# A third buffer for pair maxima, identity products moved behind a dense piece, and squares parted from their relu, in a fused top-k attention and squared-relu kernel

## The chip, the cores and the metric

The kernel runs on one core of one Trainium2 chip. A core has TensorE (PE in the profile, with its weight loads as PEld), VectorE (DVE), ScalarE (ACT), GpSimd (POOL) and SyncE (SP), which here only starts transfers. The metric is the device time of one execution in microseconds (us), the median of several runs. Lower is better.

## What is computed

For each of 8 x 8 heads with 576 rows of 64, scores are formed, all but the 32 largest of a row are dropped, and a softmax weighs the values. The result, as 4608 rows of 512, goes through two dense layers with a squared relu between them. Cut to what matters:

```python
scores = scale * np.matmul(q, k.transpose(0, 1, 3, 2))
kth = np.partition(scores, -32, axis=-1)[..., -32:-31]
scores = np.where(scores >= kth, scores, -1e9)
attn = softmax(scores)
x = np.matmul(attn, v)          # as (4608, 512)
h = np.maximum(x @ w_in, 0.0)   # w_in 512 x 2048
out = (h * h) @ w_out           # w_out 2048 x 512
```

## The kernel before

The attention is cut into 144 steps. A step is two blocks of 128 query rows (two heads of a pair, for one chunk c of the rows; a leftover chunk of 64 rows takes two pairs at once), each with 576 scores per row. The list `steps` (line 168) goes through the batches; U is 144, Z is 125, DEEP is 9. The loop of line 662 runs steps 0 to 124, the loop of line 750 the steps of the last batch, and what follows is written out by hand. Every instruction is pinned, so each engine executes its instructions in the order in which the Python code issues them. There is no scheduler to reorder them. What is decided by a planner is small: the two counters `debt` estimate how busy GpSimd and ScalarE are, and choose whether some small jobs go to one or the other engine (lines 223, 242, 504).

The pieces of a step that matter here:

- `scores` (line 193): TensorE forms the right half of the scores in the PSUM bank pair `sc_b` and the left half in `sc_a`. ScalarE copies both into the SBUF tile `s` (line 208), first the right half, `copy(1)`, then the left, `copy(0)`. In between, while the next step's right half has just been formed, TensorE also multiplies the upper half of `tops` of the step before with an identity (lines 202 to 204), which puts it into a spare region of `sc_b` called `far` (line 97).
- `split` (line 221): VectorE takes the elementwise maximum of the left half, still in `sc_a`, and the right half, in `s`, into the tile `tops` (line 231). In 131 steps this is one instruction for all 288 pairs (the step is marked `lent`, and its upper half is brought to `far` by the identity products); in 13 it is three smaller ones, which write `far` directly (lines 233 to 236).
- `join` (line 240): VectorE takes maxima, and in some steps minima, of `far` and the lower half of `tops` into `cat` (line 246). So `cat` begins with maxima of four scores each.
- `joint_mins` and `small_mins` (lines 248, 255): GpSimd computes the minima that belong to these maxima, as integer sum minus maximum. It reads `tops` (lines 252, 260), and line 253 reads the first quarter of `cat`.
- `topk` (line 268): VectorE finds the 32 largest in four rounds of eight, with a MAX8 (line 278) and a replace (line 282) for each head, over windows of `cat` that grow from 104 to 576 elements.
- `below` and `expo` (lines 322, 330): ScalarE computes the marks of dropped scores and the exponentials; GpSimd adds both (`mask`, line 326), SyncE transposes them by a transfer (`turn`), TensorE multiplies with the values (`products`, line 645), VectorE inverts the sums (line 396), and ScalarE puts the result into `x_tok` (line 421).
- The dense layers run as pieces between these: `up` (line 488, TensorE at line 495), then on ScalarE a relu into `rl` (line 501), then a square into `h2`, 82 times on ScalarE (line 506) and otherwise on GpSimd (line 509); `down` (line 517) multiplies with `w_out`, and ScalarE copies the result out. `dense` (line 558) issues one or two pieces, or an idle piece that only keeps TensorE running (line 542). A relu that is due waits in the list `late` until the next `flush` (line 346).

In the steps from 12 to 124, the order of issue is: first `below` of the step before, `split(u+2)`, `scores(u+3)`, `topk` round 0, placing of finished rows, GpSimd's minima, a dense piece, second `below`, `topk` rounds 1 to 3, `join(u+2)`, exponentials and mask of the step before, another dense piece, value products of step u-3. In the loop of line 750 the scores come after the mask, then the value products, one piece, the last rounds of `topk`, `join`, and two or three pieces.

`tops` has two buffers, so `split(u)` has to wait until the readers of `tops` of step u-2 are done. `s` has five buffers, `cat` three, `x_tok` eight.

Of the kernel before, what the change touches and what calls it, by code (L numbers as in the profile page):

```python
# [22 lines left out]
def kernel(  # L23
# [169 lines left out]
    def scores(u):  # L193
        for j in (1, 0):
            rest = steps[u][0][1] == 4
            for x, g in ((0, 0), (1, 1), (0, 1), (1, 0)) if rest else ((0, steps[u][0][2]), (1, steps[u][1][2])):
                i, c, _ = steps[u][x]
                qkT = prep[i][0]
                r = slice(64 * g, 64 * g + 64)
                pin(nc.tensor.matmul(out=sc[j][r if rest else slice(0, 128), x, 0:HALF], lhsT=qkT[r, 0, c * 128:min(S, (c + 1) * 128)],  # L200
                                     rhs=qkT[r, 1, j * HALF:(j + 1) * HALF], start=True, stop=True))
            if j and u > 1 and "lent" in st[u - 1]:
                for x in range(2):
                    pin(nc.tensor.matmul(out=far[:, x, :], lhsT=id_f[:, :], rhs=st[u - 1]["tops"][:, x, QUAR:HALF], start=True, stop=True))  # L204
        s = scp.tile([128, 2, S], f32, name="s", bufs=5)

        def copy(j):
            pin(nc.scalar.activation(s[:, :, j * HALF:(j + 1) * HALF], sc[j][:, :, 0:HALF], AF.Copy))  # L208
        st[u] = {"s": s}
        copy(1)  # L210
        if u < 2:
            st[u]["rest"] = lambda: copy(0)
        else:
            copy(0)
        for i, c, a in steps[u]:
            qk_left[i] -= 1

    def split(u):
        d = st[u]
        lend = (2 < u < U - 20 and debt["G"] < 4.9 and debt["A"] < 5.4) or Z < u < U - 5
        cat = d["cat"] = scp.tile([128, 2, S], f32, name="cat", bufs=3)
        tops = d["tops"] = scp.tile([128, 2, HALF], f32, name="tops", bufs=2)
        one, two = sc[0][:, :, 0:HALF], d["s"][:, :, HALF:S]
# [95 lines left out]
    def below(u, x):  # L322
        d = st[u]
        pin(nc.scalar.activation(marks[u % 2][:, x, :], d["s"][:, x, :], AF.Relu, bias=d["m"][3][:, x, 7:8], scale=-1.0))  # L324

    def mask(u):
# [3 lines left out]
    def expo(u, x):  # L330
        d = st[u]
        pin(nc.scalar.activation(w_two[u % 3][:, x, 0:S], d["s"][:, x, :], AF.Exp, bias=d["low"][:, x, :], scale=DROP))

    def exps(u):
# [3 lines left out]

    late, squares = [], []
    hold = {"squares": False, "out": False}  # L340
# [72 lines left out]
    def place(u):  # L413
        for x, (i, c, a) in enumerate(steps[u]):
            b, pr = pairs[i]
            o, r = st[u]["o"][:, x, :], st[u]["r"]
            if c < 4:
                if (b, c) not in x_tok:
                    x_tok[b, c] = ffp.tile([128, 512], bf16, name="x_tok", bufs=8)
                h = 2 * pr + a  # L420
# [62 lines left out]
    def block(xt, stores):  # L483
# [4 lines left out]
        def up(f0):  # L488
            def go():
# [9 lines left out]
                def bend():  # L499
# [4 lines left out]
                    if DEEP + 15 < now[0] < Z and debt["A"] < 5.4 and debt["G"] > 5.0:  # L504
                        owe(A=0.62)
                        late.append(lambda: pin(nc.scalar.activation(h2, flat, AF.Square)))
                        return
# [154 lines left out]
    for u in range(Z):  # L662
# [18 lines left out]
        if u == DEEP + 2:  # L681
            join(u + 1)
            split(u + 2)
            ahead(u + 3)
        if ok(f) and f % 2:
            invert_two(f)
# [8 lines left out]
        elif u != DEEP + 1:  # L695
            small_mins(u + lead)
        dense(u, 0)
        if u > 0:
            below(u - 1, 1)
# [4 lines left out]
            if u == DEEP + 1:  # L704
                split(u + 2)
                small_mins(u + 2)
                ahead(u + 3)
            topk(u, (3,))
            if u == DEEP:
# [19 lines left out]
        if u == DEEP:  # L729
            small_mins(u + 2)  # L730
            ahead(u + 3)
        for _ in range(2 if u < 8 or u in (U - 22, U - 19) else 1):
            prepare(u)
# [16 lines left out]
    for u in range(Z, U - 2):  # L750
# [25 lines left out]
        if not piece():  # L776
            idle_piece()
        topk(u, (2, 3))
        join(u + 2)
# [286 lines left out]
```

## Time and profile before

| | us |
|---|---|
| median of 3 runs | 893.45 (892.72 to 898.47) |
| profiled execution | 895.84 |
| its span, from first to last instruction | 893.9 |
| VectorE busy | 852.5 (95%) |
| ScalarE busy | 816.5 (91%) |
| TensorE busy | 789.3 (88%) |
| GpSimd busy | 789.4 (88%) |
| mean granted clock of TensorE | 0.979 |

Busy time is the time in which an engine executes something. A row of the view of groups gives line, engine, operation, tiles and shapes, then busy time and mean duration in ns, then the engine's idle time just before, and what ended it. A row of the view of waits says which engine and line waited for which, with the total in us, the number of times and the longest. A row of the timeline gives start and duration in us, engine, line, operation, tiles; in brackets the idle time of the engine before it and what ended that. A row of the view by stretches gives, for a part of the span, the busy time and number of instructions of each engine, the granted clock of TensorE (PEclk, 1.00 is full), and what the DMA engines did. Neighbouring instructions on ScalarE and VectorE overlap a little in these records.

### The profile page before, as it was taken

The numbers are of one execution on the slowest core, as the hardware profiler recorded it, in microseconds if no ns is written. First come the engines' busy times: TensorE is split into PE (matmuls) and PEld (weight loads), VectorE is DVE, ScalarE is ACT, GpSimd is POOL, SyncE is SP. The second block draws the span as 40 slices with busy tenths as digits, with TensorE's granted clock in tenths as the row PEclk, the third lists the DMA queues.
The fourth block names the chain that finished last, engine by engine and source line by source line (L and its number), as shares of the span: only waits on it lengthen the run. The fifth ranks groups of instructions, "written<-read, shape, count | busy, mean of one in ns | idle before, by whom it ended". The sixth has DMA issues, their size and how long they took to land.

```text
span 893.9 us, 19858 instructions
## 1 busy us (share of the span) xinstructions
PE 789.3 (88%) x5950; PEld 485.6 (54%) x6030; DVE 852.5 (95%) x3455; ACT 816.5 (91%) x1617; POOL 789.4 (88%) x745
## 2 busy tenths in 40 slices
PE   6999997889888888899889888898998998999975
PEld 3455555556555555555555555555555654656654
DVE  5999999999999999999999999999999989999994
ACT  3888999899999999999999999999999999888973
POOL 3778999999999999999999999999999878999861
PEclk8999999999999999999999999999999989999999
DMA  5597875754555556355555554455565554423431
GB/s 119 127 219 158 176 164 104 117 102 98 102 106 106 117 118 116 67 108 118 118 117 111 107 116 91 97 111 117 118 124 111 104 95 92 81 61 81 71 82 43
DMA packets 325443, 98.05 MB, mean 110 GB/s; under 512 B 317520, under 2 KB 317776, under 8 KB 325328
## 3 DMA queue, kind: packets, MB, share of 16 engines
q1 hardware_dynamic: 323984, 96.28, 53.3%
q8 instruction: 49, 0.80, 0.4%
q10 hardware_dynamic: 1344, 0.43, 0.2%
q14 instruction: 66, 0.54, 0.2%
HBM read 36.70 MB, written 9.44 MB: 52 GB/s over the span
## 4 chain that ended last, share of the span: by engine, by line
DVE 48%; PE 19%; POOL 10%; ACT 9%; issue 6%; DMA 2%; SPq 0%; POOLq 0%; ACTq 0%; DVEq 0%
DVE m L278 20%; DVE cat L282 16%; DVE tops L231 6%; DVE cat L246 4%; PE av_ps L393 3%; PE sc_b L200 3%; PE gen L495 3%; ACT s L208 2%; PE sc_b L204 2%; PE sc_a L200 2%; POOL cat L259 2%; PE dn_ps L545 2%; PE dn_ps L523 2%; POOL cat L260 2%; ACT marks_b L324 1%
## 5 line engine op out<-in xcount | busy, mean ns | idle before, releaser
L278 DVE MAX8 m<-cat 128x8 f32<-128x104 f32 (+3 forms) x1152 | 444.0, 433 | 0.0
L282 DVE MATCH_REPLACE8 cat<-m,cat 128x104 f32<-128x104 f32 (+2 forms) x864 | 265.7, 320 | 0.3 <-issue 0.3
L260 POOL TENSOR_TENSOR cat<-cat,tops 128x576 int32<-128x576 int32 (+1 forms) x144 | 195.0, 1354 | 13.0 <-DVE tops L234 1.8
L259 POOL TENSOR_TENSOR cat<-s 128x576 int32<-128x576 int32 (+1 forms) x144 | 195.0, 1354 | 6.5 <-ACT s L208 6.5
L393 PEld LDWEIGHTS <-wT 128*128 128x128 bf16 (+3 forms) x1600 | 97.5, 99 | 93.9 <-issue 51.1
L200 PE MATMUL sc_b<-qkT 64*128 64x288 f32 (+1 forms) x640 | 121.1, 454 | 29.4 <-DVE cat L246 20.9
L523 PE MATMUL dn_ps<-w_out,h 128*128 128x512 bf16 x494 | 132.4, 384 | 11.4 <-issue 5.6
L495 PEld LDWEIGHTS <-w_in 128*128 128x128 bf16 x1344 | 111.5, 98 | 45.0 <-issue 19.3
L495 PE MATMUL gen<-xT,w_in 128*128 128x256 bf16 (+1 forms) x1088 | 128.6, 266 | 1.3 <-ACT xT L455 0.7
L200 PE MATMUL sc_a<-qkT 64*128 64x288 f32 (+1 forms) x640 | 117.5, 453 | 0.0
L208 ACT ACTIVATE s<-sc_b 128x576 f32<-128x576 f32 x144 | 92.9, 645 | 26.6 <-PE sc_b L204 12.7
L324 ACT ACTIVATE marks_a<-s,m 128x576 bf16<-128x576 f32 x144 | 111.7, 784 | 0.0
L324 ACT ACTIVATE marks_b<-s,m 128x576 bf16<-128x576 f32 x142 | 109.6, 780 | 0.0
L231 DVE TENSOR_TENSOR tops<-sc_a,s 128x576 f32<-128x576 f32 x131 | 99.7, 761 | 5.3 <-POOL cat L252 4.0
L208 ACT ACTIVATE s<-sc_a 128x576 f32<-128x576 f32 x144 | 93.7, 651 | 11.1 <-PE sc_a L200 7.4
L204 PE MATMUL sc_b<-tops,id_f 128*128 128x144 f32 x524 | 101.7, 318 | 0.9 <-DVE tops L231 0.9
L204 PEld LDWEIGHTS sc_b<-tops,id_f 128*128 128x128 f32 x524 | 73.0, 193 | 54.0 <-DVE m L278 20.7
L246 DVE TENSOR_TENSOR cat<-sc_b,tops 128x288 f32<-128x288 f32 x217 | 92.1, 456 | 5.2 <-ACT s L208 5.1
L523 PEld LDWEIGHTS <-h 128*128 128x128 bf16 x560 | 48.1, 98 | 69.0 <-issue 31.2
L501 ACT ACTIVATE rl<-gen 128x512 f32<-128x512 f32 x140 | 83.3, 595 | 2.4 <-PE gen L495 2.4
L200 PEld LDWEIGHTS sc_b<-qkT 64*128 64x128 f32 (+1 forms) x640 | 49.1, 178 | 55.4 <-DVE cat L246 26.5
L282 DVE MATCH_VALUE_LOAD cat<-m,cat 128x8 f32 x864 | 75.8, 88 | 0.0
(137 smaller groups left out, 1319.4 us busy)
## 6 DMA issues: line engine op xcount, KB each, us to landing
out_dram<-wide SPq DMA_DIRECT2D x31, 256.0 KB, 2.6
q_raw<-in_q_dram SPq DMA_DIRECT2D x30, 256.0 KB, 3.6
k_raw<-in_k_dram SPq DMA_DIRECT2D x30, 256.0 KB, 3.7
v_raw<-in_v_dram SPq DMA_DIRECT2D x30, 256.0 KB, 4.1
h<-in_moe_w_in_dram SPq DMA_DIRECT2D x8, 512.0 KB, 5.3
h<-in_moe_w_out_dram SPq DMA_DIRECT2D x8, 512.0 KB, 4.3
out_dram<-wide SPq DMA_DIRECT2D x9, 128.0 KB, 2.4
q_raw<-in_q_dram SPq DMA_DIRECT2D x32, 32.0 KB, 3.1
```

The costliest lines, as they stand in the source:

```text
L200: pin(nc.tensor.matmul(out=sc[j][r if rest else slice(0, 128), x, 0:HALF], lhsT=qkT[r, 0, c * 128:min(S, (c + 1) * 128)], rhs=qkT[r, 1, j ...
L204: pin(nc.tensor.matmul(out=far[:, x, :], lhsT=id_f[:, :], rhs=st[u - 1]["tops"][:, x, QUAR:HALF], start=True, stop=True))
L208: pin(nc.scalar.activation(s[:, :, j * HALF:(j + 1) * HALF], sc[j][:, :, 0:HALF], AF.Copy))
L231: pin(tt(tops[:, :, :], one, two, op=ALU.max))
L246: pin(nc.vector.tensor_tensor(d["cat"][:, :, lo:lo + QUAR], far, d["tops"][:, :, 0:QUAR], op=op))
L259: pin(nc.gpsimd.tensor_tensor(at, s[:, :, 0:n].bitcast(i32), s[:, :, HALF:HALF + n].bitcast(i32), op=ALU.add))
L260: pin(nc.gpsimd.tensor_tensor(at, at, d["tops"][:, :, 0:n].bitcast(i32), op=ALU.subtract))
L278: pin(nc.vector.max(out=m[r][:, x, :], in_=cat[:, x, at]))
L282: pin(nc.vector.match_replace(out=cat[:, x, at], in_to_replace=m[r][:, x, :], in_values=cat[:, x, at], imm_value=NEG))
L324: pin(nc.scalar.activation(marks[u % 2][:, x, :], d["s"][:, x, :], AF.Relu, bias=d["m"][3][:, x, 7:8], scale=-1.0))
L495: pin(nc.tensor.matmul(out=hp[:, n * n_rows:(n + 1) * n_rows], lhsT=w_in[:, kh, (f0 + n) * 128:(f0 + n + 1) * 128], rhs=xt(kh), start=(kh ...
L523: pin(nc.tensor.matmul(out=op[:, :], lhsT=held["h2"][:, f, c * 128:(c + 1) * 128], rhs=w_out[:, f, :], start=(f == 0), stop=(f == NF - 1)))
```

## The change

Three edits. The tile `tops` gets a third buffer, and `x_tok` gives one up. The identity products leave `scores` for a function `bring`, which is called behind the first dense piece of a step (and at the matching places of the first steps and of the loop of line 750), so that they come after both halves of the scores and after that piece. A square that goes to ScalarE is no longer issued right behind its relu but by `follow`, which the next `below` or `expo` calls after its own instruction.

```diff
@@ scores
-            if j and u > 1 and "lent" in st[u - 1]:
-                for x in range(2):
-                    pin(nc.tensor.matmul(out=far[:, x, :], lhsT=id_f[:, :], rhs=st[u - 1]["tops"][:, x, QUAR:HALF], start=True, stop=True))
+    def bring(w):
+        if w > 0 and "lent" in st[w]:
+            for x in range(2):
+                pin(nc.tensor.matmul(out=far[:, x, :], lhsT=id_f[:, :], rhs=st[w]["tops"][:, x, QUAR:HALF], start=True, stop=True))
@@ split
-        tops = d["tops"] = scp.tile([128, 2, HALF], f32, name="tops", bufs=2)
+        tops = d["tops"] = scp.tile([128, 2, HALF], f32, name="tops", bufs=3)
@@ below and expo, at the end of each
+        follow()
@@
-    late, squares = [], []
+    late, later, squares = [], [], []
+
+    def follow():
+        while later:
+            later.pop(0)()
@@ place
-                    x_tok[b, c] = ffp.tile([128, 512], bf16, name="x_tok", bufs=8)
+                    x_tok[b, c] = ffp.tile([128, 512], bf16, name="x_tok", bufs=7)
@@ bend
-                        late.append(lambda: pin(nc.scalar.activation(h2, flat, AF.Square)))
+                        later.append(lambda: pin(nc.scalar.activation(h2, flat, AF.Square)))
@@ loop of steps 0 to Z-1
             ahead(u + 3)
+            bring(u + 2)
...
         dense(u, 0)
+        if u and not DEEP < u < DEEP + 3:
+            bring(u + lead)
...
                 ahead(u + 3)
+                bring(u + 2)
...
             ahead(u + 3)
+            bring(u + 2)
@@ loop of steps Z to U-3
         products(u - 2)
         if not piece():
             idle_piece()
+        bring(u + 2)
         topk(u, (2, 3))
         join(u + 2)
```

More of the change, by code (lines that the diff above doesn't have):

```diff
@@ L332, in expo @@
         pin(nc.scalar.activation(w_two[u % 3][:, x, 0:S], d["s"][:, x, :], AF.Exp, bias=d["low"][:, x, :], scale=DROP))
+        follow()
     def exps(u):
```

## The prediction

> **What bounds the kernel now.** The page comes first, then busy time by stretch. The span is cut at 24, 100, 757, 830 and 870 us: start, weight loading, the long middle, the last batch's loop from line 750, the tail.
>
> ```profile
> span 893.9 us, 19858 instructions
> ```
>
> ```profile
> core 0: us, PE busy (x) PEld busy (x) DVE busy (x) ACT busy (x) POOL busy (x), PEclk, DMA share, GB/s
> 24.00:100.00 76.00, 72.25 (x465) 37.98 (x470) 73.93 (x294) 64.63 (x120) 62.20 (x54) 1.00 0.80 177
> 100.00:757.00 657.00, 582.37 (x4371) 360.81 (x4429) 646.12 (x2633) 637.62 (x1265) 618.51 (x572) 0.98 0.55 110
> 757.00:830.00 73.00, 68.44 (x555) 43.93 (x562) 67.99 (x280) 62.28 (x128) 69.00 (x60) 0.98 0.33 69
> ```
>
> In the middle VectorE (DVE) works 646.1 of 657 us, ScalarE (ACT) 637.6, GpSimd (POOL) 618.5. VectorE sets the pace; ScalarE is 8.5 us behind it. VectorE's own work is unchanged: in the built programs its instructions, GpSimd's and SyncE's stand in the same order before and after. So the change can only act on VectorE's idle time, and the middle holds 657 - 646.1 = 10.9 us of that. The waits of VectorE in that stretch say whom it waits for:
>
> ```profile
> DVE tops L231 <- POOL cat L252: 4.0, 8, 1.4
> DVE shares L404 <- PE av_ps L393: 2.8, 4, 2.2
> DVE cat L246 <- ACT s L208: 1.7, 3, 0.9
> DVE tops L231 <- ACT s L208: 0.9, 3, 0.5
> ```
>
> 4.0 us is what the third buffer aims at, 1.7 + 0.9 = 2.6 us what a lighter ScalarE could give back, 2.8 us is TensorE's. A gain of 1% is 8.9 us, about what a measurement of this kernel can tell from no change; 4.0 + 2.6 = 6.6 does not reach it.
>
> **Third buffer for the pair maxima (line 225).** It removes the wait of split for the reader of the tile two steps back. The longest of the eight:
>
> ```profile
> 234.34 0.80 POOL L252 TENSOR_TENSOR cat<-tops 128x288 int32<-128x288 int32 x1
> ...
> 235.17 0.76 DVE L231 TENSOR_TENSOR tops<-sc_a,s 128x576 f32<-128x576 f32 x1 [1.35 <-POOL cat L252]
> ...
> 235.22 0.79 POOL L253 TENSOR_TENSOR cat<-cat 128x288 int32<-128x288 int32 x1
> ...
> 236.29 0.25 DVE L282 MATCH_REPLACE8 cat<-m,cat 128x104 f32<-128x104 f32 x1
> ```
>
> What is late next stands in the same rows: L253 reads the first quarter of cat, which L282 overwrites. L253 ends at 236.01; L282 started at 236.29. So the replace may move up by 0.28 us, not by 1.35, and the rest becomes a wait of L282 for L253. Eight times 0.28 is 2.2 us at most if GpSimd keeps its time; all 4.0 if it comes earlier; 0 if its lag sits elsewhere. GpSimd does come a little earlier, since it waits for ScalarE's exponentials and 33 of the 82 squares now stand behind the second of these instead of between the two. I take -2.5 us. The tile x_tok pays with one buffer of its eight. A batch fills four, so at seven a buffer returns seven fillings later, by when the tile before it has long been transposed: 0 (bounds 0 and, should SyncE's queue be late once, +0.5).
>
> **Squares apart from their relu (lines 339, 506).** All 82 squares leave the place right behind their relu:
>
> ```profile
> L506 ACT ACTIVATE h<-rl 128x512 bf16<-128x512 f32 x82 | 51.8, 632 | 2.6
> ```
>
> ```profile
> 403.81 0.57 ACT L501 ACTIVATE rl<-gen 128x512 f32<-128x512 f32 x1
> ...
> 404.42 0.63 ACT L506 ACTIVATE h<-rl 128x512 bf16<-128x512 f32 x1
> ...
> 404.96 0.58 ACT L135 ACTIVATE qkT<-gen 128x512 f32<-128x512 f32 x1
> ...
> 405.43 0.77 ACT L324 ACTIVATE marks_b<-s,m 128x576 bf16<-128x576 f32 x1
> ```
>
> Relu to square takes 404.42 - 403.81 = 0.61 us from start to start; the equally long copy L135 hands over in 405.43 - 404.96 = 0.47, since there nothing is needed from the instruction before. The square pays 0.14 us each time: 82 x 0.14 = 11.5 us off ScalarE's 637.6. On VectorE's path only the 2.6 us above can come back; bounds 0 and -2.6, and I take -1.5, because part of the 2.6 belongs to stretches where TensorE, not ScalarE, was late. In 49 of the 82 cases the square now stands between line 324 and the copy of sc_b. It was ahead of both before, so that copy is no later. A square comes out later by up to a microsecond; the down product that reads it stands pieces behind and, in the built program, no down product waits for a ScalarE square by itself: 0 (up to +0.5 if one piece came to wait).
>
> **Identity products behind the first dense piece (lines 202 to 204 into bring).** 131 pairs of matmuls move; no DMA does. Their work is the same, their neighbours change. The copy of sc_b no longer waits for them, so ScalarE gains some of this:
>
> ```profile
> ACT s L208 <- PE sc_b L204: 12.7, 18, 1.5
> ```
>
> But the join (L246) still needs them, and all three parts of a bank are kept apart: in the built program the moved product waits for ScalarE's copy of sc_b, and the join for the moved product as well as the copy. Before, the join followed the copy at once:
>
> ```profile
> 325.99 0.64 ACT L208 ACTIVATE s<-sc_b 128x576 f32<-128x576 f32 x1
> ...
> 326.66 0.46 DVE L246 TENSOR_TENSOR cat<-sc_b,tops 128x288 f32<-128x288 f32 x1 [0.49 <-ACT s L208]
> ```
>
> Copy end 326.63, join 326.66. Now the product, 0.76 us by the rows below, stands between them with a second hand-over: 0.03 + 0.76 + 0.03, so about 0.8 us more, up to 1.2 if the 0.39 us that TensorE loses ahead of such weights counts too. What is queued behind the waiting product on TensorE is the second dense piece, the value products and the next scores; these wait for ScalarE's x_tok copy anyway, which follows the same copy of sc_b, so I charge them nothing extra. Followed through the timeline, 41 of the 112 joins from 98 to 751 us start less than 0.9 us behind the end of the copy, the first and the last of them these:
>
> ```profile
> 113.98 0.64 ACT L208 ACTIVATE s<-sc_b 128x576 f32<-128x576 f32 x1
> ...
> 115.39 0.47 DVE L246 TENSOR_TENSOR cat<-sc_b,tops 128x288 f32<-128x288 f32 x1
> ...
> 736.97 0.65 ACT L208 ACTIVATE s<-sc_b 128x576 f32<-128x576 f32 x1
> ...
> 738.09 0.45 DVE L246 TENSOR_TENSOR cat<-sc_b,tops 128x288 f32<-128x288 f32 x1
> ```
>
> They are bunched in some seven bouts in which ScalarE falls behind. If ScalarE fell behind as before, each bout would cost up to 0.8 once: 7 x 0.8 = 5.6 us. It does not: 0.14 us a square over eight to ten squares a bout is 1.1 to 1.4 us more room than the 0.8 taken. I take +1.0 for the bouts where TensorE is late instead, bounds 0 and +5.6.
>
> By the Trainium skill, page PSUM — Partial Sum Buffer, section PSUM bank collisions raise a hardware error, any two engines must be kept apart on one bank, whatever columns they touch. By that rule nobody could drop the new wait while far lies in sc_b's bank; the trace agrees with a join that reads other columns than the copy and yet waits for it, and the sum stays the one made here from rows.
>
> Two places show a price that ScalarE's room doesn't pay. At the start, TensorE is the chain:
>
> ```profile
> 45.23 0.76 PE L200 MATMUL sc_b<-qkT 64*128 64x288 f32 x4 [0.87 <-ACT qkT L146]
> ...
> 45.91 0.76 PE L204 MATMUL sc_b<-tops,id_f 128*128 128x144 f32 x4
> ...
> 46.60 0.76 PE L200 MATMUL sc_a<-qkT 64*128 64x288 f32 x4
> ...
> 47.29 2.12 PE L545 MATMUL dn_ps<-fill,id_h 128*128 128x512 bf16 x7
> ...
> 47.44 0.82 DVE L246 TENSOR_TENSOR cat<-sc_b,tops 128x288 f32<-128x288 f32 x2
> ```
>
> L545 is two idle pieces of 1.06. In the new order sc_a ends at 46.67, the first idle piece at 47.7, the product at 48.4: the join comes 1.0 us later than 47.44. TensorE's pace is unchanged, so this shifts VectorE once: +0.9 (bounds 0 and +1.5).
>
> In the last batch's loop the product stands behind products and a piece:
>
> ```profile
> 826.73 0.76 PE L200 MATMUL sc_b<-qkT 64*128 64x288 f32 x4
> ...
> 827.41 0.76 PE L204 MATMUL sc_b<-tops,id_f 128*128 128x144 f32 x4
> ...
> 828.79 0.79 PE L393 MATMUL av_ps<-vau_a,wT 128*128 128x65 bf16 x10
> ...
> 828.89 0.82 DVE L246 TENSOR_TENSOR cat<-sc_b,tops 128x288 f32<-128x288 f32 x2 [1.02 <-ACT s L208]
> ...
> 829.74 0.81 PE L523 MATMUL dn_ps<-w_out,h 128*128 128x512 bf16 x3 [0.16 <-issue]
> ```
>
> Same work, product last: it ends where L523 ends now, 830.55, and the join starts at 830.6 instead of 828.89: 1.7 us later. TensorE works 68.4 of 73 us here and has two or three pieces to do before it needs that join, so the delay does not repeat. It is one shift, +1.6 us (bounds 0, if VectorE catches up in the tail, and +2.4), and nothing behind hides it.
>
> **Sum.** -2.5 - 1.5 + 1.0 + 0.9 + 1.6 = -0.5 us. The profiled execution took 895.84 us (1.9 around its span), so 895.3 for one like it; it lies 2.4 above the median of 893.45, and against the median I predict 893.0.
>
> **Rivals.** *Slower:* ScalarE's 11.5 us are eaten elsewhere (its lag comes from what it waits for) and the product behind the copy sets every tight join. It speaks for it that ScalarE waits for TensorE too:
>
> ```profile
> ACT s L208 <- PE sc_a L200: 7.4, 16, 0.6
> ```
>
> Price 5.6 for the bouts, 1.5 and 2.4 at the ends, gains halved (-2): 893.45 + 7.5 = 901; beyond 1% once the bouts cost over 7 us. *Faster:* GpSimd and ScalarE come early enough to clear all 6.6 us of the middle, and the ends cost 1.0: 888. For it stands ScalarE's room, against it L253 above. *The clock:* TensorE's granted clock falls to half after some poorly filled windows:
>
> ```profile
> 514.30:517.70 3.40, 1.64 (x16) 0.82 (x15) 3.40 (x11) 3.40 (x9) 3.32 (x4) 1.00 0.51 113
> 517.70:521.10 3.40, 3.40 (x22) 2.09 (x20) 3.40 (x19) 3.33 (x8) 3.32 (x4) 0.51 0.32 63
> 719.10:725.90 6.80, 6.80 (x26) 3.56 (x26) 6.28 (x26) 5.83 (x12) 6.46 (x8) 0.50 0.50 78
> ```
>
> A wait in the middle of a step splits TensorE's idle time, and windows could fill better or worse. The stretch at 719 cost VectorE 6.80 - 6.28 = 0.5 itself and at most the 2.2 us wait in the L404 row behind it. Two more such stretches give 893.0 + 5 = 898, two fewer 888. The Trainium skill, page TensorE: Matmul & The Clock Gate, section Part 1: The HAM clock gate (the "warmup" mystery), asks for an idle window of about 3.4 us; the trace differs, the window at 514.3 was busy 1.64 of 3.40 us. By the page's rule a step that never idles that long could not change the clock at all.
>
> **How the numbers follow.** Forecast 0.56 (its own range 889.5 to 896.5), slower rival 0.20, faster rival 0.16, clock 0.08. Half of the slower rival passes 902.4 (1% over), and a little of the clock: 0.11. A fifth of the faster one passes 884.5: 0.03. The remaining 0.86 is within 1%. The range takes the faster rival's 888 less a microsecond of its bounds and the slower one's 901: 887 to 901.
>
> **What would show it.** Right: the tops row for L252 gone, a new, shorter wait of L282 for L253; relu to next instruction 0.47; a join waiting for the product at line 221, in the first 60 us and from 757; VectorE busy 852.5 as before. Wrong: VectorE's idle time in the middle above 12 us with joins waiting for line 221 throughout (then the room argument fails), or under 5 us (then L253 was no limit).

## The result and the profile after

The changed kernel takes 885.01 us (median of 5 runs, 881.30 to 886.72), the kernel before in the same session 893.45 (5 runs, 891.56 to 899.90). The ratio is 0.9881, with a 95% interval of 0.9832 to 0.9931. Run again beside later experiments it took 882.41 us against 896.80, ratio 0.9841 (0.9802 to 0.9881). So it is 1.2 to 1.6% faster. Predicted were 893.0 us, a range of 887 to 901, and 0.03 for faster by over 1%: the prediction was wrong.

The profiled execution took 881.3 us, the fastest of its five; the profiled one of the kernel before, 895.84, lies above its median. So the two traces differ by more than the medians. From the page of the changed kernel:

```profile
span 879.4 us, 20006 instructions
...
PE 767.8 (87%) x6030; PEld 483.7 (55%) x6030; DVE 849.1 (97%) x3455; ACT 804.6 (91%) x1617; POOL 788.5 (90%) x745
```

ScalarE's 816.5 us of work became 804.6, and VectorE's 852.5 became 849.1. The view by stretches, cut as before:

```profile
24.00:100.00 76.00, 70.95 (x476) 40.14 (x476) 74.02 (x298) 64.42 (x122) 63.00 (x54) 0.98 0.81 178
100.00:757.00 657.00, 573.88 (x4510) 362.85 (x4507) 653.89 (x2678) 637.35 (x1286) 628.03 (x584) 0.99 0.57 112
757.00:830.00 73.00, 69.32 (x615) 47.74 (x614) 69.50 (x285) 63.55 (x130) 68.95 (x59) 0.98 0.35 71
```

In the middle VectorE is now idle for 657 - 653.89 = 3.1 us instead of 10.9, and in the same time it issues 2678 instructions instead of 2633. Most of the gain lies there. All that VectorE waits for in that stretch, by the view of waits:

```profile
DVE cat L248 <- PE sc_b L221: 2.2, 1, 2.2
```

The waits for GpSimd (4.0 us), for ScalarE (2.6) and for the value products (2.8) are gone; one wait for a moved product is new. ScalarE's own waits in that stretch:

```profile
ACT s L205 <- DVE cat L284: 7.7, 6, 2.6
ACT s L205 <- PE sc_a L200: 3.0, 9, 0.8
```

Before, no row of the first kind stood above 0.4 us in the middle. It does not mean what its name says. A wait for several engines is put down to the one that came last, and the place at 234 us shows the order:

```profile
231.97 0.80 DVE L248 TENSOR_TENSOR cat<-sc_b,tops 128x288 f32<-128x288 f32 x2
...
232.83 1.19 PE L200 MATMUL sc_b<-qkT 64*64 64x288 f32 x8 [1.37 <-DVE cat L248]
...
234.12 0.65 ACT L205 ACTIVATE s<-sc_b 128x576 f32<-128x576 f32 x1 [1.36 <-DVE cat L284]
```

TensorE may form the next right half only when VectorE's join has read `sc_b` (or, in a step that is not lent, when its split has written there): here it starts 0.06 us behind the join's end at 232.77. The copy starts 0.10 us behind the end of these scores at 234.02. In all 11 idle times above 0.15 us ahead of this copy in the middle the order is the same. So ScalarE has run ahead until only VectorE's hold on `sc_b` stops it. The five buffers of `s` are not the limit.

The place of the longest wait that the prediction quoted (1.35 us at 235.17) shows how far GpSimd has come forward. From the timeline of the changed kernel:

```profile
229.90 0.80 POOL L254 TENSOR_TENSOR cat<-tops 128x288 int32<-128x288 int32 x1
...
230.78 0.80 POOL L255 TENSOR_TENSOR cat<-cat 128x288 int32<-128x288 int32 x1
...
232.69 0.75 DVE L233 TENSOR_TENSOR tops<-sc_a,s 128x576 f32<-128x576 f32 x1
```

Before, the split stood idle until GpSimd's add ended at 235.14. Now the add ends 2.0 us and the subtract behind it 1.1 us before the split starts, and the replace that the prediction named as the next limit (line 284 here) starts at 233.80, 2.2 us behind the subtract. With the third buffer alone the add at this place ended at 234.41 and the split started at 234.40: GpSimd was still late.

### The profile page after: what moved, and what is told of

It reads as the page before. It is cut to its first block, busy times and chain, and to the rows that moved or that the text cites. A ratio compares the mean times of both kernels' runs of the same rounds, so it can differ in the third digit from the quotient of the medians.

```text
span 879.4 us, 20006 instructions
## 1 busy us (share of the span) xinstructions
PE 767.8 (87%) x6030; PEld 483.7 (55%) x6030; DVE 849.1 (97%) x3455; ACT 804.6 (91%) x1617; POOL 788.5 (90%) x745
## 4 chain that ended last, share of the span: by engine, by line
DVE 65%; PE 18%; issue 8%; ACT 4%; POOL 2%; DMA 2%; SPq 0%; DVEq 0%; ACTq 0%; POOLq 0%
DVE m L280 28%; DVE cat L284 19%; DVE cat L248 8%; DVE tops L233 7%; PE gen L504 4%; PE dn_ps L532 4%; PE sc_b L200 3%; PE sc_b L221 2%; PE sc_a L200 2%; PE av_ps L402 2%; ACT s L205 1%; DMA wT<-w_two_b 1%; DVE sc_b L235 1%; PE dn_ps L554 1%; POOL cat L261 1%
## 5 line engine op out<-in xcount | busy, mean ns | idle before, releaser
L280 DVE MAX8 m<-cat 128x8 f32<-128x104 f32 (+3 forms) x1152 | 437.2, 421 | 0.1
L284 DVE MATCH_REPLACE8 cat<-m,cat 128x104 f32<-128x104 f32 (+2 forms) x864 | 261.4, 310 | 0.1
L262 POOL TENSOR_TENSOR cat<-cat,tops 128x576 int32<-128x576 int32 (+1 forms) x144 | 194.9, 1353 | 15.5 <-DVE tops L236 2.9
L200 PE MATMUL sc_b<-qkT 64*128 64x288 f32 (+1 forms) x640 | 118.2, 452 | 64.1 <-DVE cat L248 49.1
L532 PE MATMUL dn_ps<-w_out,h 128*128 128x512 bf16 x560 | 145.2, 385 | 3.8 <-ACT wide L542 3.7
L326 ACT ACTIVATE marks_a<-s,m 128x576 bf16<-128x576 f32 x144 | 115.3, 809 | 0.0
L221 PE MATMUL sc_b<-tops,id_f 128*128 128x144 f32 x524 | 94.7, 304 | 22.4 <-ACT s L205 21.7
L200 PE MATMUL sc_a<-qkT 64*128 64x288 f32 (+1 forms) x640 | 112.4, 434 | 0.1
L221 PEld LDWEIGHTS sc_b<-tops,id_f 128*128 128x128 f32 x524 | 75.4, 193 | 57.5 <-ACT s L205 52.2
L233 DVE TENSOR_TENSOR tops<-sc_a,s 128x576 f32<-128x576 f32 x131 | 97.6, 745 | 0.0
L430 ACT ACTIVATE x_tok<-av_ps,shares 128x64 bf16<-128x64 f32 x254 | 67.7, 333 | 11.6 <-DVE shares L407 11.2
```

Source lines behind the costliest of these rows:

```text
L233: pin(tt(tops[:, :, :], one, two, op=ALU.max))
L262: pin(nc.gpsimd.tensor_tensor(at, at, d["tops"][:, :, 0:n].bitcast(i32), op=ALU.subtract))
L280: pin(nc.vector.max(out=m[r][:, x, :], in_=cat[:, x, at]))
L284: pin(nc.vector.match_replace(out=cat[:, x, at], in_to_replace=m[r][:, x, :], in_values=cat[:, x, at], imm_value=NEG))
L532: pin(nc.tensor.matmul(out=op[:, :], lhsT=held["h2"][:, f, c * 128:(c + 1) * 128], rhs=w_out[:, f, :], start=(f == 0), stop=(f == NF - 1)))
```

## The experiments

Beside the kernel before, twelve kernels were run: the changed one, run twice, and eleven others. VectorE executes the same instructions in the same order in all of them, so the traces can be compared between the same two instructions: those that the kernel before starts at 100, 757 and 870 us. The table gives the time between their starts with VectorE's idle time in brackets (from one execution of each kernel), the ratio to the kernel before with its interval, and the margin: the median, over steps 15 to 121, of the time from the end of the copy of `sc_b` to the start of the join. A caution on the middle column: 2.3 us of the 657.1 are the wait for the value products at 728 us, behind a stretch of half the clock. No other execution has it, not even that of the third buffer alone. And a caution on the medians: the kernels were run in several sessions, in which the kernel before took 893.45 to 898.05 us; each ratio is to the kernel before in the same session, so the ratios compare better than the medians.

| kernel | median us | ratio | middle (idle) | last batch (idle) | margin |
|---|---|---|---|---|---|
| before | 893.45 | | 657.1 (10.8) | 113.0 (5.2) | 1.16 |
| third buffer alone | 895.48 | 0.9989 (0.9966 to 1.0013) | 655.5 (9.5) | 115.6 (7.7) | 1.37 |
| squares alone | 889.71 | 0.9935 (0.9907 to 0.9963) | 647.3 (2.9) | 114.7 (6.8) | 1.83 |
| squares in place, other input | 887.80 | 0.9892 (0.9865 to 0.9919) | 648.1 (3.3) | 113.6 (5.6) | 1.59 |
| products moved alone | 889.53 | 0.9917 (0.9886 to 0.9948) | 650.5 (5.3) | 111.2 (3.8) | 1.89 |
| no products | see below | | 651.2 (5.8) | 111.4 (3.8) | 1.51 |
| changed, products behind the scores | 899.27 | 1.0019 (0.9996 to 1.0042) | 662.6 (15.5) | 110.8 (3.7) | 1.98 |
| changed less squares | 887.41 | 0.9883 (0.9852 to 0.9914) | 650.2 (5.1) | 110.6 (3.3) | 1.95 |
| changed less products moved | 886.11 | 0.9879 (0.9845 to 0.9912) | 647.5 (2.8) | 111.8 (4.3) | 1.67 |
| changed less third buffer | 884.17 | 0.9848 (0.9817 to 0.9878) | 647.4 (3.3) | 111.8 (4.6) | 2.62 |
| changed, loop early | 884.52 | 0.9858 (0.9830 to 0.9886) | 646.6 (2.2) | 112.1 (4.5) | 2.64 |
| loop early, two buffers | 884.84 | 0.9859 (0.9822 to 0.9896) | 645.9 (1.7) | 112.1 (4.5) | 2.68 |
| changed | 885.01 | 0.9881 (0.9832 to 0.9931) | 647.2 (3.0) | 110.9 (3.8) | 2.57 |
| changed, again | 882.41 | 0.9841 (0.9802 to 0.9881) | 648.1 (3.8) | 110.7 (3.4) | 2.65 |

Where the product stands behind the copy, the margin cannot fall below the product's own time of some 0.7 us plus two hand-overs, so small margins are ruled out there by the order itself. What the product then costs is read from the joins that wait for it.

By these cuts the 14.5 us between the two traces are 0.6 in the start, 9.9 in the middle, 2.1 in the last batch and 1.9 in the tail.

The theories: A, ScalarE's relief by the parted squares ends its lag, and with it GpSimd's, whose masks wait for exponentials. B, the third buffer clears the waits for GpSimd. C, the moved products let ScalarE run ahead. They were first told apart by doing one part alone.

### Squares alone

```diff
     pin(nc.scalar.activation(marks[u % 2][:, x, :], d["s"][:, x, :], AF.Relu, bias=d["m"][3][:, x, 7:8], scale=-1.0))
+        follow()
...
     pin(nc.scalar.activation(w_two[u % 3][:, x, 0:S], d["s"][:, x, :], AF.Exp, bias=d["low"][:, x, :], scale=DROP))
+        follow()
...
-                        late.append(lambda: pin(nc.scalar.activation(h2, flat, AF.Square)))
+                        later.append(lambda: pin(nc.scalar.activation(h2, flat, AF.Square)))
```

> The kernel before with the squares parted from their relu, and nothing else (two buffers for the pair maxima, identity products in the scores). Theory A (ScalarE's relief of some 11.5 us ends its lag, and with it GpSimd's, whose masks wait for exponentials): most of the gain of 8.4 us, 886 to 889 us; VectorE's waits of its pair maxima for GpSimd (4.0 us before) fall under 1.5 us although there are still two buffers, and its waits for ScalarE (2.6 us) under 1. Theory B (the third buffer clears the waits for GpSimd): 890 to 892, waits for GpSimd still 3 us or more. Theory C (the moved identity products let ScalarE run ahead): 891 to 893.5, the margin between copy of sc_b and join stays near 1.2 us.

Measured: 889.71 us, ratio 0.9935. The margin rose from 1.16 to 1.83 us, and the middle lost nearly all of its idle time. VectorE's waits in the middle:

```profile
DVE cat L246 <- ACT s L208: 2.5, 3, 1.4
DVE tops L231 <- ACT s L208: 0.5, 1, 0.5
DVE sc_b L233 <- ACT x_tok L428: 0.5, 1, 0.5
```

There is no wait for GpSimd any more, with two buffers. At the place at 235 us:

```profile
233.11 0.80 POOL L252 TENSOR_TENSOR cat<-tops 128x288 int32<-128x288 int32 x1
...
235.08 0.75 DVE L231 TENSOR_TENSOR tops<-sc_a,s 128x576 f32<-128x576 f32 x1
```

GpSimd's add ends at 233.91, 1.2 us before the split needs it. Why GpSimd came forward is seen in its masks' waits for the exponentials in the middle. First the kernel before, then squares alone:

```profile
POOL w_two_a L328 <- ACT w_two_a L332: 8.3, 8, 4.1
POOL w_two_b L328 <- ACT w_two_b L332: 5.8, 10, 1.1
POOL w_two_c L328 <- ACT w_two_c L332: 4.1, 6, 1.4
```

```profile
POOL w_two_b L329 <- ACT w_two_b L333: 2.8, 6, 0.7
POOL w_two_a L329 <- ACT w_two_a L333: 2.4, 5, 1.1
POOL w_two_c L329 <- ACT w_two_c L333: 1.4, 3, 0.8
```

The sum falls from 18.2 to 6.6 us. One wait of 4.1 us among the 18.2 stands at 735 us, behind a stretch of half the clock; the third buffer alone, which does not have it, still has 13.3. So theory A holds and B falls. The time came out just above A's 886 to 889, and the waits for ScalarE did not fall below 1 us: three joins still waited for its copy, one of them, 1.4 us at 756, in what the table counts as the last batch. Yet between the same instructions of the middle the waits for ScalarE fell only from 2.6 to 1.6 us, while the 4.0 us for GpSimd and the 2.8 for the value products (2.3 of them the wait at 728 us) nearly all went. Theory C expected a margin near 1.2 us here, and missed.

### Third buffer alone

```diff
-        tops = d["tops"] = scp.tile([128, 2, HALF], f32, name="tops", bufs=2)
+        tops = d["tops"] = scp.tile([128, 2, HALF], f32, name="tops", bufs=3)
...
-                    x_tok[b, c] = ffp.tile([128, 512], bf16, name="x_tok", bufs=8)
+                    x_tok[b, c] = ffp.tile([128, 512], bf16, name="x_tok", bufs=7)
```

> The kernel before with a third buffer for the pair maxima and seven for x_tok, and nothing else. Theory A: within 1.5 us of the kernel before (892 to 893.5), with the waits of VectorE for GpSimd gone from the pair maxima but come back at the first replace of a step (it waits for GpSimd's subtract in the same tile) or as waits for ScalarE. Theory B: 888.5 to 890, with these waits gone and nothing in their place. Theory C: no change.

Measured: 895.48 against 895.61 us for the kernel before, run beside it, ratio 0.9989 with 1 inside its interval. The largest rows of VectorE's waits in the middle:

```profile
DVE shares L404 <- PE gen L143: 1.7, 1, 1.7
DVE shares L404 <- ACT rl L501: 1.4, 1, 1.4
DVE cat L282 <- POOL cat L253: 1.3, 3, 0.8
DVE tops L231 <- ACT s L208: 1.3, 2, 0.8
```

Here is the wait that the prediction foretold, the replace for GpSimd's subtract: 1.3 us, 3 times, in place of the 4.0 us of the splits. Two single waits of its reciprocals, 1.7 and 1.4 us, are new. The margin of 1.37 us is not far from the 1.16 before. The buffer takes a wait away and leaves the lag.

### Products moved alone

```diff
-            if j and u > 1 and "lent" in st[u - 1]:
-                for x in range(2):
-                    pin(nc.tensor.matmul(out=far[:, x, :], lhsT=id_f[:, :], rhs=st[u - 1]["tops"][:, x, QUAR:HALF], start=True, stop=True))
...
         dense(u, 0)
+        if u and not DEEP < u < DEEP + 3:
+            bring(u + lead)
...
             idle_piece()
+        bring(u + 2)
```

> The kernel before with the identity products moved behind the first dense piece, and nothing else. Theory A: ScalarE lags as before and the join now also waits for the product, so no gain or a small loss, 893 to 898. Theory B: the same. Theory C: 887 to 890, with the waits of ScalarE's copy of sc_b for the identity products (12.7 us) gone and the margin between that copy and the join near 2 us or more.

Measured: 889.53 us, ratio 0.9917; margin 1.89 us. So theory C holds too. Theory A, which for this kernel said no gain, was wrong here; the relief of ScalarE by the squares and that by the products are two sources of the same thing. The rows of ScalarE's two copies in the middle, as the view of groups gives them with their idle time ahead, for the kernel before and then for this one:

```profile
L208 ACT ACTIVATE s<-sc_a 128x576 f32<-128x576 f32 x112 | 72.8, 650 | 5.7 <-PE sc_a L200 5.2 <-DVE cat L282 0.4
L208 ACT ACTIVATE s<-sc_b 128x576 f32<-128x576 f32 x112 | 72.0, 643 | 8.1 <-ACT marks_a L324 3.7 <-PE sc_b L204 2.8 <-issue 1.1
```

```profile
L205 ACT ACTIVATE s<-sc_a 128x576 f32<-128x576 f32 x113 | 73.6, 651 | 2.8 <-PE sc_a L200 2.4 <-DVE cat L284 0.3
L205 ACT ACTIVATE s<-sc_b 128x576 f32<-128x576 f32 x113 | 72.6, 642 | 4.3 <-DVE cat L284 2.6 <-ACT marks_a L326 0.7 <-DVE m L280 0.5
```

ScalarE stood idle ahead of its copies for 8.1 + 5.7 = 13.8 us before and 4.3 + 2.8 = 7.1 now, though the names of the releasers mislead here too. In the kernel before, each of the 13 idle times above 0.15 us ahead of the copy of `sc_b`, 7.6 us in all, ends 0.04 to 0.09 us behind the end of the product, whoever is named. In this kernel 6 are left, 4.2 us in all, and each ends 0.05 to 0.10 us behind the scores, which TensorE could start only when VectorE's join or split had let go of `sc_b`. So ScalarE is early there. Both halves profit: the copy of `sc_b` no longer waits for the product, and `sc_a` is formed sooner. The product is not free at the join:

```profile
DVE cat L248 <- PE sc_b L221: 3.1, 5, 2.4
```

VectorE's idle time in the middle fell all the same, from 10.8 to 5.3 us.

### One part taken away from the changed kernel

The three edits shown above undone one at a time; in each kernel the other two stay. For the squares only this line goes back:

```diff
-                        later.append(lambda: pin(nc.scalar.activation(h2, flat, AF.Square)))
+                        late.append(lambda: pin(nc.scalar.activation(h2, flat, AF.Square)))
```

> The changed kernel with the pair maxima back to two buffers and x_tok to eight. Theory A and C together (relief of ScalarE, by the parted squares and by the moved products, each worth about 6 us alone): 884 to 888 us, and VectorE's pair maxima wait for GpSimd under 0.7 us in all. Theory B, in the form left after the first three runs (the third buffer pays once the other limits are gone): 888 or more, with these waits back at 2 us or more.

> The changed kernel with each square again right behind its relu. If parting the squares and moving the products clear the same waits, one is nearly enough: 885 to 888 us. If each brings its own 6 us: 889 to 891, near the 889.5 of the moved products alone. ScalarE busy 811 to 813 us, as with the moved products alone (811.9); median margin from the copy of sc_b to the join about 1.9 us, as there.

> The changed kernel with the identity products back inside the scores, between the two halves. If the same waits are cleared by either: 885 to 888 us. If each brings its own: 888.5 to 891, near the 889.7 of the parted squares alone. Margin from the copy of sc_b to the join about 1.8 to 2.0 us.

Measured: 884.17, 887.41 and 886.11 us. Without the third buffer nothing is lost, and no split waits for GpSimd: theory B falls in its second form too. Without the squares ScalarE works 811.2 us and the margin is 1.95, as for the products alone; without the moved products the margin is 1.67, below the 1.8 to 2.0 expected. In the middle, 647.5 us without the products moved stand against 647.2 with them: where the squares have cleared the waits, moving the products adds next to nothing there. The other way round, 650.2 become 647.2. So in the middle both clear the same waits, and the squares are enough. What the products add then lies in the last batch, 111.8 against 110.9 and 110.7 by single executions; over the whole run the intervals of the two kernels overlap, so that gain is not shown. Over the whole run the medians do not tell a sum from an overlap: 0.65 + 0.83 + 0.11 = 1.59% for the parts alone, against 1.19 and 1.59% in the two measurements of the whole.

### Products directly behind the scores

```diff
             ahead(u + 1 + lead)
+            if u:
+                bring(u + lead)
...
         dense(u, 0)
-        if u and not DEEP < u < DEEP + 3:
-            bring(u + lead)
```

> The changed kernel with the identity products directly behind both halves of the scores, ahead of the first dense piece, in the loop of steps 0 to 124 (the loop of the last batch as changed). If the gain comes from freeing the two copies of ScalarE (Theory C): no more than 2 us from the changed kernel, 883 to 888, with the margin from copy to join at 2.3 us or more. If the dense piece in front matters (the product waits for the copy of sc_b and holds TensorE, so that pieces, value products and the copies behind them come late): 889 or more, with TensorE waiting at the identity product for ScalarE for 60 us or more in the middle and a margin under 2 us.

Measured: 899.27 us, ratio 1.0019: the whole gain is lost, though the margin is 1.98 and ScalarE waits no longer ahead of its copies than in the changed kernel (8.0 us in the middle against 12.9). The waits of TensorE's weight loads in the middle, for this kernel and then for the changed one:

```profile
PEld sc_b L221 <- ACT s L205: 135.5, 106, 2.2
```

```profile
PEld sc_b L221 <- ACT s L205: 48.7, 70, 1.7
```

The length of this wait does not decide by itself: it is 86.6 us with the products moved alone, which gain. It matters what stands behind it. ScalarE's largest wait in the middle of this kernel, and VectorE's:

```profile
ACT qkT L135 <- PE gen L131: 16.4, 25, 1.2
```

```profile
DVE cat L248 <- PE sc_b L221: 6.4, 10, 1.2
DVE shares L413 <- PE gen L143: 2.6, 4, 1.3
DVE shares L413 <- PE av_ps L402: 2.6, 7, 0.5
```

The product must wait for ScalarE's copy of `sc_b`, and TensorE's queue stands still behind it. Transposes come late: ScalarE waits 16.4 us for them, where it waited 1.2 in the kernel before and 1.1 in the changed one. Pieces and value products come late too, and VectorE's joins and reciprocals wait. With the piece in front, TensorE does useful work while ScalarE copies. In this pair of kernels moving the products is worth its gain only with that cover, and the second expectation held.

### What in the squares it was

Parting the squares changes two things: the hand-over from relu to square, and the place. To tell them apart, the square stayed in its place but read the relu result of the piece before, so its output is not the right one.

```diff
-    late, squares = [], []
+    late, squares, done_rl = [], [], []
...
-                        late.append(lambda: pin(nc.scalar.activation(h2, flat, AF.Square)))
+                        read = done_rl[0] if done_rl else rl
+                        done_rl[:] = [rl]
+                        other = read[:, :].rearrange("p (n r) -> p n r", n=per)
+                        late.append(lambda: pin(nc.scalar.activation(h2, other, AF.Square)))
                         return
+                    done_rl[:] = [rl]
```

> The kernel before, in which each of ScalarE's 82 squares reads the relu result of the dense piece before instead of its own; place and size of the square are unchanged, and what the dense layers compute is not what the reference asks. It takes away what the square needs from the instruction just before it, and nothing else. Theory D (the gain of the parted squares is this hand-over, 0.14 us each): 888 to 891 us, ScalarE busy 805 to 808, relu to square 0.47 us from start to start. Theory E (the gain comes from the later place, which lets marks, exponentials and copies go ahead of the square): 894 to 897, ScalarE busy 811 or more or, if busy falls all the same, no gain from it.

Measured: 887.80 us, ratio 0.9892, ScalarE busy 806.2 us. From its timeline:

```profile
403.50 0.57 ACT L501 ACTIVATE rl<-gen 128x512 f32<-128x512 f32 x1
403.98 0.62 ACT L509 ACTIVATE h<-rl 128x512 bf16<-128x512 f32 x1
```

0.48 us from start to start, where it was 0.61. Over all 82 squares the median was 0.62 us before and is 0.48 here; 0.48 is also what a relu takes before any other instruction. Theory D holds: the hand-over is the price, and the later place adds nothing to the time that can be measured. The place is not without effect: here 1.2 us of VectorE's waits for GpSimd are left in the middle, and none with the squares parted. The Trainium skill, page Perfetto Trace Analysis, section Optimizing Scalar/DVE Operations, says that the write-acknowledgement half of an operation's profiled latency overlaps with the next instruction. The trace agrees for a square that reads another tile: it starts 0.09 us before the relu's record ends. One that reads its own starts 0.04 us behind it, so there the overlap is lost.

### Products earlier in the last batch

The changed kernel had two joins that waited 2.2 us, at 746 and 773 us. The first in its timeline:

```profile
743.41 1.89 PE L532 MATMUL dn_ps<-w_out,h 128*128 128x512 bf16 x4
...
745.10 1.02 PE L221 MATMUL sc_b<-tops,id_f 128*128 128x144 f32 x4
...
746.22 0.82 DVE L248 TENSOR_TENSOR cat<-sc_b,tops 128x288 f32<-128x288 f32 x2 [2.23 <-PE sc_b L221]
```

```profile
743.00:745.30 2.30, 2.30 (x10) 1.23 (x11) 0.99 (x3) 1.03 (x2) 2.30 (x4) 0.50 0.01 4
```

The piece of four matmuls, which takes 1.03 or 1.04 us in 134 of 140 such pieces, took 1.89 there, at a granted clock of 0.50. The experiment puts the product ahead of it:

```diff
         products(u - 2)
+        bring(u + 2)
         if not piece():
             idle_piece()
-        bring(u + 2)
```

> The changed kernel with the identity products of the last batch's loop ahead of its first dense piece (behind the value products). If the two waits of 2.2 us at 746 and 773 us are the price of a piece in front of the product (it takes 1.9 us there at the half clock), they shrink by 1 to 2 us each: 880 to 884 us against 885. If the reciprocals or the exponentials behind the join take the place of these waits: 884 to 887, no gain.

Measured: 884.52 us; between the same instructions 112.1 us against 110.9. The two waits became 1.27 and 0.53 us, and others, of 1.15 us and less, came up in the steps behind. No gain: the second expectation held.

### Without the products, and the changed kernel again

```diff
-            if j and u > 1 and "lent" in st[u - 1]:
-                for x in range(2):
-                    pin(nc.tensor.matmul(out=far[:, x, :], lhsT=id_f[:, :], rhs=st[u - 1]["tops"][:, x, QUAR:HALF], start=True, stop=True))
```

> The kernel before without the identity products: the join reads what was left in the spare region, so the maxima of the upper half are not the right ones; every other instruction stays. It shows what the products cost where they stood. Theory F (their cost is that ScalarE's two copies stand behind them, and moved behind the dense piece they cost nothing more): as with the moved products alone, 888 to 891 us, margin from copy to join 1.8 us or more. Theory G (the moved products still cost something on TensorE or at the join): 885 or less, at least 3 us better than the moved products alone. If ScalarE's copies were not held by them: 893 or more.

This kernel took 4706 us, which no theory had expected. The kernel ends with a test of its own sums, and where rows are off it computes everything again in a slower way; false maxima set this off. Only its first pass can be read. There, between the same instructions, the middle took 651.2 us and the last batch 111.4, as with the moved products alone (650.5 and 111.2). That speaks for theory F: what the products cost lay in their place, and behind a piece they cost no more than if they were not there. It is a weak comparison, since TensorE has less to do here and its clock was lower (0.94 in the middle against 0.99), and the margin of 1.51 us is not the 1.8 that F asked for:

```profile
100.00:757.00 657.00, 534.98 (x4024) 321.13 (x4023) 650.87 (x2652) 637.55 (x1274) 621.73 (x578) 0.94 0.55 111
```

At the end the changed kernel was run once more, with no edit, and beside it a kernel with the earlier place in the last batch, as above, and two buffers:

```diff
-        tops = d["tops"] = scp.tile([128, 2, HALF], f32, name="tops", bufs=3)
+        tops = d["tops"] = scp.tile([128, 2, HALF], f32, name="tops", bufs=2)
...
-                    x_tok[b, c] = ffp.tile([128, 512], bf16, name="x_tok", bufs=7)
+                    x_tok[b, c] = ffp.tile([128, 512], bf16, name="x_tok", bufs=8)
...
+        bring(u + 2)
         if not piece():
             idle_piece()
-        bring(u + 2)
```

> The changed kernel with two buffers for the pair maxima and the identity products of the last batch's loop ahead of its first dense piece. If the third buffer is worth nothing with the other two parts in place, and the earlier place in the loop nothing either: within 2 us of the changed kernel run beside it. If both small differences of the earlier runs were real: 881 to 883.

> The changed kernel itself, run beside the other two so that they have it on the same chip: 883 to 887 us.

Measured: 884.84 and 882.41 us beside each other, ratios 0.9859 and 0.9841. No version beats the changed kernel by more than can be measured; the third buffer could be given back to `x_tok` at no cost that was measured.

## Why the prediction was wrong, point by point

**What bounds the kernel.** That VectorE sets the pace and that the change can act only on its 10.9 us of idle time in the middle was right in the main: 7.8 us of them went, 2.3 of which are the wait at 728 us that no other execution has. Beyond the prediction, 2.1 us came from shorter records of VectorE itself, for which no run shows a cause, and the last batch gave 2.1 more (113.0 to 110.9). What failed was the next step, to take each row of the waits as the share of one cause: 4.0 us to the third buffer, 2.6 to ScalarE, 2.8 to TensorE. The waits for GpSimd were late exponentials at one remove. Squares alone, with two buffers, cleared them all.

**Third buffer, -2.5 us.** It showed no gain, alone or in company. The interval alone, -0.34 to +0.13% or -3.0 to +1.2 us, does not rule the -2.5 out; but without the buffer the changed kernel took 884.17 us, no more than with it. The mechanism, that line 253 would be late next, was right for a kernel in which GpSimd keeps its lag, and the third buffer alone shows just that wait. In the changed kernel GpSimd leads by a microsecond or more, so neither the buffer nor that limit matters. The section Optimization Strategy of the page Perfetto Trace Analysis of the Trainium skill says that a gap that repeats on the engine that should be saturated can mean too few buffers. The trace agrees that such a gap was there, eight times; here it was the reader of the buffer that was late, not the buffer that was missing.

**Squares, -1.5 us.** The price was nearly right: 0.14 us each, 11.5 in all forecast, and ScalarE's busy time fell from 816.5 to 806.4, by 10.1. The step that failed is "On VectorE's path only the 2.6 us above can come back". Measured alone: 0.65% or 5.8 us (interval 0.37 to 0.93%), and of the 2.6 us themselves 1.6 stayed. What came back stood to other names, the 4.0 us of GpSimd above all. The reading that fits: an engine 1.3% less busy than the one that sets the pace is late in bouts, 0.14 us a square shortens them, and GpSimd, which waits for ScalarE's exponentials, comes earlier too (its waits for them fell from 18.2 to 6.6 us).

**Products, bouts +1.0 us.** The sign was wrong: alone they gained 0.83% or 7.4 us (0.52 to 1.14%). The prediction had both sides before it, the 12.7 us that ScalarE waits for the products over the whole run and the 0.8 us that a join would wait longer, and charged only the second. That charge did fall due, at 5 joins and 3.1 us in the middle with the products moved alone, and at one of 2.2 us in the changed kernel. But joins so close behind the copy that they must wait had become rare, since ScalarE came earlier: before, 39 of 107 steps had a margin under 0.9 us. The step that failed is to put the relief of ScalarE's copies at nothing. Charging nothing for what is queued behind the waiting product fits the kernel without the products, a weak comparison as said; the kernel with the products directly behind the scores shows what that queue costs without a piece in front, some 12 to 16 us by the ratios.

**Products, start +0.9 and last batch +1.6 us.** In both places the step that failed is the shift itself: it was worked out from where TensorE stood before, and TensorE did not stay there. In the start the same step reads after the change:

```profile
43.48 0.76 PE L200 MATMUL sc_b<-qkT 64*128 64x288 f32 x4 [0.87 <-ACT qkT L146]
...
45.53 0.65 PE L221 MATMUL sc_b<-tops,id_f 128*128 128x144 f32 x4
...
47.52 0.80 DVE L248 TENSOR_TENSOR cat<-sc_b,tops 128x288 f32<-128x288 f32 x2
```

The scores began at 43.48 instead of 45.23, so the product ended at 46.18, 1.3 us ahead of the join, which did not wait. Two other joins, at 75.0 and 92.1 us, did wait 0.5 and 1.0 us longer than before, but waits of reciprocals went; VectorE is 0.6 us earlier at 100 us. In the last batch the prediction stood on TensorE's position at 826.73. The same step before and after:

```profile
825.01 0.75 DVE L278 MAX8 m<-cat 128x8 f32<-128x256 f32 x2
```

```profile
812.62 0.76 PE L200 MATMUL sc_b<-qkT 64*128 64x288 f32 x4
...
813.10 0.74 DVE L280 MAX8 m<-cat 128x8 f32<-128x256 f32 x2
...
815.38 0.65 PE L221 MATMUL sc_b<-tops,id_f 128*128 128x144 f32 x4
...
816.15 0.82 DVE L248 TENSOR_TENSOR cat<-sc_b,tops 128x288 f32<-128x288 f32 x2 [0.20 <-PE sc_b L221]
```

The scores began 826.73 - 825.01 = 1.7 us behind VectorE's third round before, and 0.5 us ahead of it after. TensorE had come 2.2 us forward, so the join waited 0.20 us for the product, where it had waited 1.02 for ScalarE. In the last batch the kernels with moved products took 110.6 to 112.1 us between the same instructions, those with the products in their old place 111.8 to 115.6.

**The rivals.** The faster one, 888 at a chance of 0.16, named what happened: GpSimd and ScalarE come early enough to clear the middle. It was held down by L253, which was no limit (the idle time under 5 us that the prediction named as the sign of this came true), and priced too high by the 1.0 us for the ends and by leaving out the waits for TensorE. The slower one fell: ScalarE's room was not eaten. The clock does not explain the gain either: in the second execution of the changed kernel the mean granted clock of the middle was 0.98, as before, and the middle took 648.1 us against 657.1. Runs with a mean clock from 0.977 to 0.982 have a median of 885.0 us with the change (7 runs) and 895.1 without (27). Of the signs of being right, the row for L252 went and a relu hands over in 0.48 us; the wait for L253 came with the third buffer alone and not in the changed kernel, no join in the first 60 us waits for the product, and VectorE's busy time fell to 849.1 us.

## What to carry to other kernels

When an engine is nearly as busy as the one that sets the pace, do not price its relief by the waits that stand to its name: follow who is late because of it (here GpSimd's masks, then VectorE's splits), and count every wait on that chain. A wait for a buffer's reader is first a question about the reader; run the cheap test of the buffer alone. An instruction that must wait for another engine wants useful work in front of it in its own queue: the same two matmuls differ by some 12 to 16 us between one place and the next.

## What was not expected of the hardware

The runs of one kernel spread with TensorE's granted clock. In 62 runs of the kernel before, from 891.8 to 901.7 us, the 21 with a mean clock of 0.974 or less have a median of 898.3 us and the 12 with 0.981 or more one of 894.0, although VectorE and not TensorE sets the pace. In a half-clock stretch a piece took 1.89 us instead of 1.04, as at 743 us above, and the join behind it waited 2.2 us. The other join that waited 2.2 us, at 773 us, stands behind such a stretch too (granted clock 0.55 from 770 to 773.5). That single executions of the last batch differ by a microsecond or two fits this, but no run separates it; small differences between these kernels stay open.
